# A first token list made in two parts, with its first 768 rows fetched under a narrower wait, and bracket counts kept from the search rounds

## The chip, the core and the metric

The kernel runs on one core of one Trainium2 chip. The metric is device time in microseconds (us) of one launch; lower is better. The time before is 1282.61 us, the median of three runs (1281.73 to 1284.68).

## What is computed

Two stages follow one another. The first is a channel attention over four batches (5056 tokens, 256 channels); the second sends every token of its output to exactly one of eight experts, in a greedy order with a fixed capacity, and runs that expert's two-layer network on it.

```python
qn = q / (np.linalg.norm(q, axis=1, keepdims=True) + 1e-06)
kn = k / (np.linalg.norm(k, axis=1, keepdims=True) + 1e-06)
s = kn.transpose(0, 2, 1) @ qn / tau
...
x = v @ a                                  # softmax of s; 4 x 5056 tokens, 256 channels
...
cap = N // E                               # 20224 tokens / 8 experts = 2528
logits = x @ w_gate
order = np.argsort(-logits.flatten())
for idx in order:                          # largest logit first
    tok, e = idx // E, idx % E
    if assigned[tok] >= 0 or counts[e] >= cap: continue
    assigned[tok] = e; counts[e] += 1
for e in range(E):
    mask = assigned == e
    out[mask] = np.maximum(x[mask] @ w1[e], 0.0) @ w2[e]
```

## The kernel before

**Attention and values.** `scores` and `softmax` make the four attention matrices. `x_tiles` (matmul L225, copy out of PSUM by ScalarE at L229) then multiplies values by them, eight 128-token rows at a time for each (batch, chunk) pair, and `store_x` (L235) sends the rows to a DRAM buffer `x_d` through ScalarE's DMA queue, four token rows per store. The last thirteen chunks stand in `TODO`; its last two are (2,4) and (3,0). They are computed while the first expert's tokens are being chosen. For the very last half chunk the loop stores two token rows at a time instead of four.

**Choosing the tokens of an expert (`route`).** The reference's greedy loop is done one full expert at a time, in eight passes p = 0 to 7; R = 8 - p experts are still open in pass p. A pass seeks the 32-bit score at which the first open expert is full. It is a search in eight rounds of four bits, four on the high half of the key and four on the low half. In each round VectorE compares all keys with 15 thresholds (L608), TensorE counts the hits per expert (`totals`: twenty matmuls at L577, one at L590), and VectorE reads the largest count (L597), marks the thresholds that are reached (`hit`, L601) and makes the next thresholds (L627, L634). I call the twenty-one matmuls of a round a **visit**. Behind the eight rounds stands a ninth visit: the keys are compared with the threshold that was found, once with "at least" and once with "above" (L651, L653), `totals` runs again, and from its two counts come the expert that is full and the room left in each (L658, L663). The mask of the chosen tokens follows at L719, the expert's number `ei` at L725. In the last pass (R = 1) nothing is searched.

**The list (`compact`).** From the mask a prefix sum (L514), a small matmul pair (L768, L769) and twenty tests (matmul L786, one per 128 list entries) give, for each of the 2528 list places, the row in `x_d` (`src`, L884) and in the output (`idx`, L897). For p = 0 ScalarE evaluates 11 of the tests (L804) and VectorE nine (L820); for the others ScalarE evaluates all.

**The experts.** Weights are fetched with an indirect DMA by GpSimd as soon as `ei` is known and the expert before has begun (`load_w`, L1051); the buffer of the second weight matrix must first be freed by the splitting of the previous one (L1060 on ScalarE, L1063 on VectorE). Token rows are fetched by indirect DMA, 128 per instruction (`load_x`, L1084), in chunks of up to four columns; the first expert's chunks have 2, 4, 4, 4, 4 and 2 columns (`FIRST_CUT`). The rows are turned, by TensorE for the first three chunks (`turn`: transposes L1237, ScalarE copy L1239, VectorE remainder L1242) and elsewhere by VectorE and DMA (`stage`, L1143). `layer1` (L1280, L1283, L1288) and `layer2` (L1314, L1321) then run, and GpSimd scatters the result rows (L1323).

**What sets the order.** All instructions are issued in the order in which the program emits them on their engine (`manual_schedule`). A planner (`Order`, with streams of generators) decides this order by a cost model: `ve(n)` is a VectorE instruction's cost, a yield of "P" asks for a place on TensorE, "A" on ScalarE, "W" waits for something to be emitted. Ties go to the stream with the lower priority number, and layer work comes first. A stream's next VectorE instruction is taken to be ready `DVE_TO_DVE` (70 ns) after its last.

**The seam between values and experts.** Behind the last value tile `actx.close()` gives back the buffers of the attention stage, among them the pool `vp` with the values and with the row buffers `xs` that `store_x` reads. Right after that the pool `ffx` is opened in the space that became free; `xg`, into which the rows are fetched, lies in it. The PSUM pools are exchanged in the same place.

```python
        actx.close()
        cctx.close()
        ffx = ctx.enter_context(tc.tile_pool(name="ffx", bufs=2))
        ...
        for c in range(2):
            load_x(0, c)
            while queue:
                gather()
        ...
        for i in range(START_TICKS):          # 24 matmuls on weights, result unused
            o.tick(200)
            PE.matmul(idle, lhsT=..., rhs=..., start=(i == 0), stop=(i == START_TICKS - 1))
        turn(0, 0, 0)
        turn(0, 0, 1)
```

The 24 matmuls (L1376) produce nothing. Chunk 1's transposes are emitted between `layer1(0, 0)` and `layer2(0, 0)`.

Of the kernel before, what the change touches and what calls it, by code (L numbers as in the profile page):

```python
# [8 lines left out]
F32 = mybir.dt.float32  # L9
# [21 lines left out]
LASTC = CAP - (NCOL - 1) * 128  # L31
GW = C + E
RB = 3
NACT = 11
# [14 lines left out]
HALF = 32768.0  # L49
CG = 128 // J  # L50
# [29 lines left out]
START_TICKS = 24  # L80
# [14 lines left out]
def attention_moe(ctx: ExitStack, tc: tile.TileContext, q, k, vt, tau, wg, w1t, w2t, tabs, out):  # L95
# [136 lines left out]
    def store_x(b, c, xs, t0, t1):  # L232
        r0 = (b * NCH + c) * CH
        rows = x_d[r0:r0 + CH].rearrange("(p t) c -> p t c", t=T)
        nc.scalar.dma_start(rows[:, t0:t1], xs[:, t0 % TH:t0 % TH + t1 - t0, 0:C])  # L235
# [283 lines left out]
    def route(p, R):  # L519
# [10 lines left out]
        else:  # L530
# [34 lines left out]
                            code9[:, None, 0:Q].to_broadcast([128, COLS, Q]), op=OP.is_equal)  # L565
            Ex = rtile("Ex", (128, J, E), F32R)
# [26 lines left out]
            def hits():  # L593
# [4 lines left out]
                hit = rtile("hit", (128, NT))  # L598
# [3 lines left out]
                r["n"] = n  # L602

# [8 lines left out]
            def search(keys):  # L612
                thr, cur = th0, None
                for i in range(NR):
                    yield from compare(keys, thr)
                    if 0 < i < NR - 1:
# [20 lines left out]

            yield from search(hi)
# [11 lines left out]
            yield ve(COLS, ptr=1)  # L650
            V.tensor_scalar(ge[:, :, 0], w.rearrange("p (g c) -> p g c", c=CG), th, None, op0=OP.is_ge)  # L651
            yield ve(COLS, ptr=1)
            V.tensor_scalar(ge[:, :, 1], w.rearrange("p (g c) -> p g c", c=CG), th, None, op0=OP.is_gt)  # L653
            yield from totals()
            tot = r["tot"]
            gen = rtile("gen", (128, E))
            yield ve(Q, psum=True)
            V.scalar_tensor_tensor(gen[:, 0:Q], tot[:, 0, :], 0.0, code9[:, 0:Q], op0=OP.is_ge, op1=OP.mult)  # L658
# [3 lines left out]
            yield ve(Q, psum=True)  # L662
            V.tensor_scalar(o9[:, 0, 0:Q], tot[:, 1, :], -1.0, None, op0=OP.mult)  # L663
# [57 lines left out]
        yield ve(COLS, 0.5)  # L721
        r["sc"] = prefix(r["mask"], "a")
# [6 lines left out]
        o.add(compact(p), lambda: COMPACT_PRIO)  # L729
# [26 lines left out]
    def compact(p):  # L756
        r = routed[p]
        sc = r["sc"]
# [13 lines left out]
        V.tensor_copy(first, po[:, 0:1])  # L772
        yield ve(COLS, psum=True)
        V.tensor_tensor(E_[:, 0:COLS], po[:, 128:128 + COLS], sc, op=OP.add)
        G = rtile("G", (128, NCOL * 128), BF)
        yield ve(NCOL * 128, 4, ptr=1)
        V.tensor_scalar(G, rgrid, first, None, op0=OP.is_ge)
# [4 lines left out]
        ended = []  # L782

# [5 lines left out]
        def by_act():  # L789
            todo = list(range(0, NACT, RB))  # L790
            held = []
            while todo or held:
                while todo and len(held) < 2:
                    g0 = todo.pop(0)
                    n = min(RB, NACT - g0)
# [5 lines left out]
                for i in range(n):  # L801
# [3 lines left out]
                                 accum_out=sgn[:, g0 + i:g0 + i + 1])  # L805
                yield "A", 200
                S.activation(ext[:, g0:g0 + n], pi[:, 0:n * W].rearrange("p (i w) -> p i w", w=W)[:, :, COLS:W], AF.Copy)
            ended.append(1)

        def by_dve():  # L810
            num = rtile("num", (128, NCOL))
            for g0 in range(NACT, NCOL, RB):
                n = min(RB, NCOL - g0)
# [3 lines left out]
                for i in range(n):  # L817
# [3 lines left out]
                                    op1=OP.add, accum_out=num[:, g0 + i:g0 + i + 1])  # L821
                yield ve(2 * n, psum=True)
                V.tensor_copy(ext[:, g0:g0 + n], pi[:, 0:n * W].rearrange("p (i w) -> p i w", w=W)[:, :, COLS:W])
            yield ve(NCOL)
            V.tensor_copy(at[:, NACT:NCOL], num[:, NACT:NCOL])
            ended.append(1)

        if p == 0:
# [4 lines left out]
            yield ve(NCOL)  # L833
            V.tensor_scalar(at[:, 0:NACT], sgn[:, 0:NACT], 0.5, COLS / 2.0, op0=OP.mult, op1=OP.add)
        for g in range(0, NCOL if p else 0, 2 * RB):
            yield "Q", min(2 * RB, NCOL - g) * 75
            held = []
            for g0 in range(g, min(g + 2 * RB, NCOL), RB):
                n = min(RB, NCOL - g0)
                pi = ps_t.tile([128, 512], F32, name="pt") if held else ps_c.tile([128, 512], F32, name="pi")  # L840
                tested(pi, g0, n)
# [378 lines left out]
    def turn(p, c, kb):  # L1220
# [27 lines left out]
        if kb == 1:  # L1248
            load_ahead(p, c)
# [243 lines left out]
```

## Time and profile before

| what | value |
|---|---|
| median of the three runs | 1282.61 us |
| the profiled execution, its own time | 1284.76 us |
| its span in the profile | 1282.8 us |
| mean granted TensorE clock in it | 0.997 of full speed |
| VectorE, ScalarE, GpSimd busy | 64%, 42%, 31% of the span |

The profile lists, per engine (PE is TensorE, PEld its weight loads, DVE VectorE, ACT ScalarE, POOL GpSimd, SP SyncE), when each instruction ran and what ended the idle time before it. Durations of single matmuls overlap, since TensorE pipelines them, so what a row of matmuls costs is read from the start of the next instruction. An arrow "<-" in brackets names the engine, tile and line whose end is taken to have released the wait; it is inferred from semaphores.

### The profile page before, as it was taken

What the parts mean: (1) busy time and instruction counts of PE and PEld (TensorE: products, weight loads), DVE (VectorE), ACT (ScalarE), POOL (GpSimd) and SP (SyncE); (2) the same over time, 40 slices, a digit from 0 to 9 for tenths busy, and PEclk for the clock granted to TensorE, in tenths of its full rate; (3) what the DMA queues carried; (4) which work ended last, traced back from release to release, by engine and by line L of the source; (5) the groups of instructions that cost most, each with busy time, mean ns of one, the idle gap of its engine ahead of it and who ended that gap; (6) DMA issues with size and microseconds to landing.
All of it is one profiled execution on the core that took longest, in us unless ns stands there. A gap on an engine that the chain in (4) does not pass through costs nothing.

```text
span 1282.8 us, 23360 instructions
## 1 busy us (share of the span) xinstructions
PE 1259.9 (98%) x8974; PEld 1123.1 (88%) x8974; DVE 814.9 (64%) x2013; ACT 540.3 (42%) x1217; POOL 395.4 (31%) x664
## 2 busy tenths in 40 slices
PE   7999999999899999999999999999999999999998
PEld 6889877888788989998989889988988998898998
DVE  6788596768478667867875876867644334434421
ACT  5567542335235343534442543443455333334331
POOL 1000001000343453254425533353344344335322
PEclk9999999999999999999999999999999999999999
DMA  8999982344224123232413431442243324313310
GB/s 298 365 380 340 366 324 110 132 148 185 75 84 143 49 88 114 84 91 72 161 42 95 148 102 38 143 152 70 76 147 119 111 82 144 106 63 105 111 62 33
DMA packets 67118, 178.29 MB, mean 139 GB/s; under 512 B 10944, under 2 KB 33344, under 8 KB 62400
## 3 DMA queue, kind: packets, MB, share of 16 engines
q1 hardware_dynamic: 39808, 97.54, 21.4%
q0 software_dynamic: 17664, 58.22, 13.9%
q10 hardware_dynamic: 9536, 21.06, 4.3%
q8 instruction: 70, 1.15, 0.4%
q14 instruction: 40, 0.33, 0.1%
HBM read 117.53 MB, written 59.24 MB: 138 GB/s over the span
## 4 chain that ended last, share of the span: by engine, by line
PE 85%; issue 5%; DVE 4%; DMA 2%; POOL 2%; ACT 1%; another core or an unknown queue 0%; POOLq 0%; SPq 0%; DVEq 0%; ACTq 0%
PE py L1314 31%; PE ph L1280 30%; PE s L304 8%; PE px L225 7%; PE pc L577 3%; PE px L268 2%; PE px L416 1%; POOL out_dram L1323 1%; DMA xg<-x_d,src 1%; DVE acc_q L314 1%; DVE acc_k L314 1%; DMA x_d<-xs 1%; DMA ua<-in_q_dram 1%; DVE hL L1288 0%; PE pi L786 0%
## 5 line engine op out<-in xcount | busy, mean ns | idle before, releaser
L1314 PE MATMUL py<-ua,hH 128*128 128x256 f32 (+1 forms) x2560 | 452.2, 280 | 0.0
L1280 PE MATMUL ph<-xH,ua 128*128 128x512 f32 (+3 forms) x1312 | 411.1, 388 | 4.8 <-DVE xs L1143 3.1
L1314 PEld LDWEIGHTS py<-ua,hH 128*128 128x128 f32 (+1 forms) x2560 | 389.1, 187 | 2.4
L1314 PE MATMUL py<-ua,hL 128*128 128x256 f32 (+1 forms) x1280 | 356.1, 278 | 0.0
L1288 DVE SCALAR_TENSOR_TENSOR hL<-ph,hH 128x512 fp32r<-128x512 f32 (+3 forms) x328 | 219.1, 669 | 171.8 <-ACT hH L1283 155.5
L1283 ACT ACTIVATE hH<-ph 128x512 fp32r<-128x512 f32 (+3 forms) x328 | 190.6, 582 | 235.8 <-PE ph L1280 209.3
L1280 PEld LDWEIGHTS ph<-xH,ua 128*128 128x128 f32 x1312 | 244.5, 189 | 51.4 <-DVE xs L1143 4.0
L1323 POOL DMA_INDIRECT out_dram<-y,idx x160 | 160.2, 1001 | 337.2 <-ACT y L1321 318.4
L1280 PE MATMUL ph<-xL,ua 128*128 128x512 f32 (+3 forms) x656 | 255.3, 389 | 0.8 <-DVE xL L1242 0.5
L1314 PEld LDWEIGHTS py<-ua,hL 128*128 128x128 f32 (+1 forms) x1280 | 239.1, 187 | 0.0
L1321 ACT ACTIVATE y<-py 128x256 f32<-128x256 f32 (+1 forms) x160 | 61.4, 384 | 311.2 <-PE py L1314 263.1
L1084 POOL DMA_INDIRECT xg<-x_d,src x160 | 162.5, 1016 | 94.1 <-issue 44.7
L304 PE MATMUL s<-ua 128*128 128x256 f32 (+1 forms) x640 | 145.2, 386 | 6.8 <-DMA ua<-in_q_dram 6.8
L304 PEld LDWEIGHTS s<-ua 128*128 128x128 f32 (+1 forms) x640 | 121.9, 193 | 26.7 <-issue 6.4
L1280 PEld LDWEIGHTS ph<-xL,ua 128*128 128x128 f32 x656 | 124.2, 189 | 23.4 <-DVE xL L1242 1.2
L313 ACT ACTIVATE sq<-ua 128x1024 f32<-128x1024 f32 (+1 forms) x80 | 76.3, 970 | 55.0 <-DMA ua<-in_k_dram 21.8
L1170 DVE TENSOR_TENSOR xL<-xT,xH 128x512 fp32r<-128x512 f32 (+1 forms) x68 | 44.9, 679 | 56.6 <-ACT xH L1167 56.2
L1095 POOL COPY spacer<-hH 1x1 f32<-1x1 f32 x130 | 27.1, 208 | 145.3 <-ACT hH L1283 140.1
L229 ACT ACTIVATE xs<-px 128x512 f32<-128x512 f32 x60 | 35.8, 597 | 76.2 <-PE px L225 76.2
L225 PE MATMUL px<-a,vr 128*128 128x256 f32 x256 | 59.4, 384 | 0.0
L334 POOL TENSOR_SCALAR ny<-ny 128x4 f32<-128x4 f32 x4 | 2.0, 504 | 182.8 <-ACT ny L333 182.8
L580 DVE TENSOR_TENSOR Dm<-pc,dmask 128x64 f32<-128x64 f32 (+3 forms) x63 | 12.6, 201 | 69.7 <-PE pc L577 47.2
(295 smaller groups left out, 1352.6 us busy)
## 6 DMA issues: line engine op xcount, KB each, us to landing
x_d<-xs ACTq DMA_DIRECT2D x39, 512.0 KB
ua<-in_k_dram SPq DMA_DIRECT2D x35, 512.0 KB
ua<-in_q_dram SPq DMA_DIRECT2D x35, 512.0 KB
via<-xs SPq DMA_DIRECT2D x33, 512.0 KB
xT<-via SPq DMA_DIRECT2D x132, 128.0 KB
vr<-in_vt_dram SPq DMA_DIRECT2D x14, 1024.0 KB
ua<-in_vt_dram SPq DMA_DIRECT2D x4, 1024.0 KB
xg<-x_d,src POOLq DMA_INDIRECT x160
```

Source lines behind the costliest of these rows:

```text
L225: mm = PE.matmul(px[:, i * C:i * C + width], lhsT=vs[b, c][:, kb, t + i, :], rhs=a_f[b][:, kb, 0:width], start=(kb == 0), stop=(kb == 1))
L304: newest[0] = PE.matmul(sb[:, ib * C:(ib + 1) * C], lhsT=kt[:np_, t, ib * 128:(ib + 1) * 128], rhs=qt[:np_, t, :], start=(first and t == 0 ...
L313: S.activation(sq[:n, t0:t1], t_[:n, t0:t1], AF.Square)
L577: PE.matmul(D, lhsT=ge[:, g], rhs=oh[:, cs_, 0:Q], start=(g == 0), stop=(g == COLS // CG - 1))
L1084: P.indirect_dma_start(out=xg[:n, i, :], out_offset=None, in_=x_d, in_offset=bass.IndirectOffsetOnAxis(ap=idx[:n, col:col + 1], axis=0))
L1170: V.tensor_tensor(xL[:, kb, 0:k * 128].rearrange("p (i t e) -> p i t e", i=k, t=4), rows, xH[:, kb, 0:k * 128].rearrange("p (i t e) -> p i ...
L1280: PE.matmul(ph[:, 0:nt], lhsT=l[:, w], rhs=x_[:, kb, 0:nt], start=(i == 0), stop=(i == 5))
L1283: S.activation(hH[:, fb, 0:nt], ph[:, 0:nt], AF.Relu)
L1288: V.scalar_tensor_tensor(hL[:, fb, 0:nt], ph[:, 0:nt], 0.0, hH[:, fb, 0:nt].bitcast(F32), op0=OP.max, op1=OP.subtract)
L1314: PE.matmul(py[:n, 0:C], lhsT=l[:, fb, tk], rhs=w[:, d], start=(j == 0), stop=(j == 23))
L1321: S.activation(y[:n], py[:n, 0:C], AF.Copy)
L1323: sd = P.indirect_dma_start(out=out, out_offset=bass.IndirectOffsetOnAxis(ap=idx[:n, col:col + 1], axis=0), in_=y[:n], in_offset=None)
```

## The change

**The list of expert 0 in two parts.** `compact(0)` first copies the mask without the tokens that the last one and a half chunks of values produce (all of (3,0), the second half of (2,4); `LATE_PAIR = 5`), makes a list of this reduced mask for six columns only (`HEAD = 6`, 768 places), then subtracts what is listed from the mask and makes the other 14 columns from the rest. `listed` is the old body of `compact` with a column range; three tests of the head and eight of the rest go to ScalarE. The six fetches of the head are declared independent of the stores of those last values. The last half chunk is stored with one store of four token rows.

**The ninth visit.** In each round ScalarE copies the counts out of PSUM (`S.activation(seen...)`), and a new stream `keep` runs three VectorE instructions on them: counts whose threshold was reached are shifted down by `HIT`, a minimum over the shifted ones and a maximum over the others are carried to the next round. Behind round eight the two results stand in `seen[0]`; the two comparisons and the visit are gone.

**The seam.** The 24 idle matmuls are gone. `turn_both` turns both halves of chunk 0 with four transposes in one PSUM tile. Chunk 1 is turned at steps 4 and 7 of `layer1(0, 0)`.

**Smaller edits.** The streams `compact` and `keep` are `quick` (ready without the 70 ns). `turn` first drives a list stream that reads the same PSUM tile to the end of its reading.

```diff
+            def keep():
+                for k in range(2 * NR):
+                    while len(rounds) <= k:
+                        yield "W", 0
+                    now_, then = seen[k % 2], seen[(k + 1) % 2]
+                    yield ve(NT * Q)
+                    V.scalar_tensor_tensor(now_[:, 1:NT + 1], rounds[k][:, :, None].to_broadcast([128, NT, Q]), -HIT,
+                                           now_[:, 1:NT + 1], op0=OP.mult, op1=OP.add)
+                    k0 = 0 if k else 1
+                    yield ve((NT + 1) * Q)
+                    V.tensor_reduce(then[:, 0], now_[:, k0:NT + 1].rearrange("p k r -> p r k"), axis=AX.X, op=OP.min)
+                    yield ve((NT + 1) * Q)
+                    V.tensor_reduce(then[:, NT + 1], now_[:, 1:NT + 2].rearrange("p k r -> p r k"), axis=AX.X, op=OP.max)
+                    r["kept"] = k + 1
...
+                while r["kept"] < len(rounds) - 1:
+                    yield "W", 0
+                S.activation(seen[len(rounds) % 2][:, 1:NT + 1], r["tot"][:, 0:NT], AF.Copy)
...
             th = r["cur"]
-            V.tensor_scalar(ge[:, :, 0], w.rearrange("p (g c) -> p g c", c=CG), th, None, op0=OP.is_ge)
-            V.tensor_scalar(ge[:, :, 1], w.rearrange("p (g c) -> p g c", c=CG), th, None, op0=OP.is_gt)
-            yield from totals()
+            rounds.append(r["new"])
+            while r["kept"] < 2 * NR:
+                yield "W", 0
-            V.scalar_tensor_tensor(gen[:, 0:Q], tot[:, 0, :], 0.0, code9[:, 0:Q], op0=OP.is_ge, op1=OP.mult)
+            V.scalar_tensor_tensor(gen[:, 0:Q], seen[0][:, 0], -HIT, code9[:, 0:Q], op0=OP.is_ge, op1=OP.mult)
...
     def compact(p):
+        mask = routed[p]["mask"]
+        if p > 0:
+            sc = prefix(mask, "a")
+            yield from listed(p, sc, 0, NCOL)
+            return
+        head = rtile("mem")
+        V.tensor_copy(head, mask)
+        c0 = (NCH - 1) * T + LATE_PAIR * 16
+        V.memset(head[32:64, c0:c0 + 16], 0.0)
+        V.memset(head[64:128, c0:c0 + 16], 0.0)
+        sc = prefix(head, "a")
+        yield from listed(p, sc, 0, HEAD)
+        V.tensor_scalar(sc, sc, routed[p]["first"], None, op0=OP.add)
+        V.scalar_tensor_tensor(head, sc, HEAD * 128.0, head, op0=OP.is_le, op1=OP.mult)
+        V.tensor_tensor(head, mask, head, op=OP.subtract)
+        sc = prefix(head, "a")
+        yield from listed(p, sc, HEAD, NCOL)
...
         def fetch(i, col, n):
+            rows = P.indirect_dma_start(...)
+            if p == 0 and col < HEAD:
+                for st in late_stores:
+                    tc.declare_no_dep(rows.ins, st.ins, reason="at least 768 rows of a list lie outside the last rows")
...
+    def turn_both():
+        xg = xgs[0, 0]
+        xH, xL = xts[0, 0] = (ffx.tile([128, 2, 512], F32R, name="xH"), ffx.tile([128, 2, 512], F32R, name="xL"))
+        pt = ps_t.tile([128, 512], F32, name="pt")
+        for i in range(cuts[0][0]):
+            for kb in range(2):
+                PE.transpose(pt[:, kb * nt + i * 128:kb * nt + (i + 1) * 128].bitcast(F32R),
+                             xg[:, i, kb * 128:(kb + 1) * 128].bitcast(F32R), identr)
+        for kb in range(2):
+            rows = pt[:, kb * nt:(kb + 1) * nt]
+            S.activation(xH[:, kb, 0:nt], rows, AF.Copy)
+            V.tensor_tensor(xL[:, kb, 0:nt], rows, xH[:, kb, 0:nt].bitcast(F32), op=OP.subtract)
+        o.pe += 1500
...
-                if i + 1 == len(TODO) and t >= TH:
-                    store_x(b, c, xs, t, t + 2)
-                elif t % TH == 2:
-                    store_x(b, c, xs, t - 2, t + 2)
+                if t % TH == 2:
+                    st = store_x(b, c, xs, t - 2, t + 2)
+                    if (b, c) == PAIRS[LATE_PAIR][1] or (b, c) == PAIRS[LATE_PAIR][0] and t >= TH:
+                        late_stores.append(st)
...
-        for i in range(START_TICKS):
-            o.tick(200)
-            PE.matmul(idle, lhsT=wt[0, 0][0][:, 0:128], rhs=wt[0, 0][0][:, 512:1024], start=(i == 0),
-                      stop=(i == START_TICKS - 1))
-        turn(0, 0, 0)
-        turn(0, 0, 1)
+        turn_both()
...
-            h[0] = layer1(p, 0, {**pieces} if p == 0 else {2: [turn_at(1, 0)], 7: [turn_at(1, 1)], **pieces})
+            h[0] = layer1(p, 0, {4: [turn_at(1, 0)], 7: [turn_at(1, 1)]} if p == 0 else {2: [turn_at(1, 0)], 7: [turn_at(1, 1)], **pieces})
...
-                    turn(p, 1, 0)
-                    turn(p, 1, 1)
```

More of the change, by code (lines that the diff above doesn't have):

```diff
@@ L565, in route @@
                             code9[:, None, 0:Q].to_broadcast([128, COLS, Q]), op=OP.is_equal)
+            seen = [eq.bitcast(F32).rearrange("p r c -> p (r c)")[:, i * 320:i * 320 + (NT + 2) * Q]
+                    .rearrange("p (k r) -> p k r", r=Q) for i in range(2)]
+            yield ve(Q)
+            V.tensor_scalar(seen[0][:, NT + 1], ne[:, 0, 0:Q], -1.0, None, op0=OP.mult)
+            rounds = []
+            r["kept"] = 0
+            def keep():
[12 more added lines that the diff above has]
+                    r["kept"] = k + 1
             Ex = rtile("Ex", (128, J, E), F32R)
@@ L615, in search @@
                     yield from compare(keys, thr)
+                    if r["new"] is not None:
+                        rounds.append(r["new"])
                     if 0 < i < NR - 1:
@@ L636, in search @@
                 r["cur"] = cur
+            o.add(keep(), lambda: EDGE_PRIO).quick = True
+            r["new"] = None
             yield from search(hi)
@@ L775, in compact @@
         G = rtile("G", (128, NCOL * 128), BF)
-        yield ve(NCOL * 128, 4, ptr=1)
-        V.tensor_scalar(G, rgrid, first, None, op0=OP.is_ge)
+        yield ve(nc_ * 128, 4, ptr=1)
+        V.tensor_scalar(G[:, 0:nc_ * 128], rgrid[:, 0:nc_ * 128], first, None, op0=OP.is_ge)
         W = COLS + 2
@@ L789, in by_act @@
         def by_act():
-            todo = list(range(0, NACT, RB))
+            todo = list(range(0, nact, RB))
             held = []
@@ L889, in compact @@
+        V.copy_predicated(src[:, cs_], early[:, cs_], w3_[:, cs_])
+        for col in range(c0, c1):
+            r["src", col] = src
+        if not short:
+            r["time"] = o.pe
+            done["idx", p] = True
+            lists.append(p)
         bt = rtile("bt", (128, NCOL))
-        yield ve(NCOL)
-        V.tensor_scalar(bt, src, float(NCH * CH), None, op0=OP.is_ge)
+        yield ve(nc_)
+        V.tensor_scalar(bt[:, cs_], src[:, cs_], float(NCH * CH), None, op0=OP.is_ge)
         for b_ in range(2, B):
-            yield ve(NCOL)
-            V.scalar_tensor_tensor(bt, src, float(b_ * NCH * CH), bt, op0=OP.is_ge, op1=OP.add)
@@ L901, in attention_moe @@
+        for col in range(c0, c1):
+            r["idx", col] = idx
+        if not short:
+            done["out", p] = True
+    reading = []
     spacer = rt.tile([1, 2], F32, name="spacer")
@@ L1232, in turn @@
         xH, xL = xts[p, c]
+        while reading:
+            reading[0].step()
         o.flush(turned[0])
```

149 lines of the change are left out of this document (83 added, 66 removed).

## The prediction

> **What bounds the kernel now.** I read the page's first rows and its chain of work first, then the stages by window, then the seam in order of time.
>
> ```profile
> span 1282.8 us, 23360 instructions
> PE 1259.9 (98%) x8974; PEld 1123.1 (88%) x8974; DVE 814.9 (64%) x2013; ACT 540.3 (42%) x1217; POOL 395.4 (31%) x664
> PE 85%; issue 5%; DVE 4%; DMA 2%; POOL 2%; ACT 1%; another core or an unknown queue 0%; POOLq 0%; SPq 0%; DVEq 0%; ACTq 0%
> ```
>
> TensorE is the bound nearly everywhere: 98% busy, 85% of the chain. So an edit is worth what it takes from TensorE's own work or from its few empty places. Of these the seam between values and experts is the largest behind the start:
>
> ```profile
> 287.00:322.60 35.60, 35.50 (x228) 30.33 (x226) 31.55 (x95) 19.38 (x52) 0.00 (x0) 1.00 0.50 193
> 322.60:332.06 9.46, 7.11 (x50) 5.52 (x50) 4.13 (x13) 0.98 (x2) 4.22 (x5) 1.00 0.27 91
> 332.06:343.00 10.94, 9.53 (x80) 8.89 (x79) 5.21 (x13) 3.97 (x10) 2.84 (x5) 0.84 0.12 37
> 582.31:704.25 121.94, 121.25 (x987) 109.91 (x986) 89.14 (x258) 49.32 (x126) 49.01 (x80) 1.00 0.30 95
> ```
>
> The columns behind the stretch are its length, then busy time of PE, PEld, DVE, ACT, POOL, the granted clock, DMA share and GB/s. The 7.11 us of PE in the second row are mostly the 24 idle matmuls. In the third the granted clock is 0.84: 10.94 x 0.16 = 1.75 us lost. In order of time the seam reads:
>
> ```profile
> 319.78 2.81 PE L225 MATMUL px<-a_last,vr 128*128 128x256 f32 x12
> ...
> 322.62 0.60 ACT L229 ACTIVATE xs<-px 128x512 f32<-128x512 f32 x1 [1.13 <-PE px L225]
> 323.25 0.33 ACTq L235 DMA_DIRECT2D x_d<-xs  x1
> 323.27 1.20 PE L1376 MATMUL ph<-ua 128*128 128x512 f32 x4 [0.69 <-ACT xs L229]
> ...
> 326.63 0.95 POOL L1084 DMA_INDIRECT xg<-x_d,src  x1 [40.59 <-DVE Ex L586]
> ...
> 330.64 0.28 PE L1237 MATMUL pt<-identr,xg 128*128 128x128 f32 x1 [0.74 <-DMA xg<-x_d,src]
> ...
> 332.06 0.35 PE L1280 MATMUL ph<-xH,ua 128*128 128x256 f32 x1
> ...
> 342.60 0.53 PE L1237 MATMUL pt<-identr,xg 128*128 128x128 f32 x4 [1.28 <-DVE xL L1242]
> ```
>
> I call the end of the last value matmul T = 319.78 + 2.81 = 322.59. The first fetch starts 4.04 us later, the second column's rows are there at T + 8.05, layer 1 starts at T + 9.47. The DVE instruction that the fetch's row names belongs to pass 1 and writes nothing that the fetch reads, and the fetch's list had long been ready (its row is below): what it waited for is the last store, issued at 323.25.
>
> **Does the fetch really go ahead?** That decides 10 us, so it comes first. The change takes away the dependence of the six fetches on the last stores through `x_d`. But there is a second one. `xg` lies in `ffx`, opened in space that `vp` has just given back, and two rows show what a first instruction in such a new pool waits for:
>
> ```profile
> L904 POOL MEMSET ge<- 128x2560 bf16 x1 | 2.2, 2231 | 26.1 <-DVE L L421 26.1
> ```
>
> The memset of `ge`, the first one in the pool `rt`, waits 26.1 us for a DVE copy out of `turned`. It shares no data with it; what they have in common is that `turned` belongs to a pool that was closed just before. Likewise the first idle matmul above (323.27) reads only weights and still waits for ScalarE's last copy out of `px`, a tile of the closed PSUM pool. So a new pool's tiles wait for the last users of the closed pools. The users of `vp` are the last value matmuls, ScalarE's last copy into `xs`, and the last stores that read `xs`. The diff leaves `ffx` and its place as they are, and a declared independence of two DMAs doesn't speak of pools. I forecast that **the fetches still start behind the last store**, and the list's two parts buy nothing.
>
> **The sum, part by part.**
>
> *Ninth visit.* The chain of waits in the value stage gives the price of a visit:
>
> ```profile
> 221.03 14.01 PE px L225 x64
> ...
> 242.18 3.07 PE px L225 x14
> 245.25 0.58 PE pc L577 x20
> 245.84 1.38 PE px L225 x6
> 247.21 0.06 PE pc L590
> 247.27 3.07 PE px L225 x14
> ...
> 893.20 0.51 PE pc L577 x20
> ...
> 899.50 0.51 PE pc L577 x20
> ```
>
> From 242.18 to 247.27 are 5.09 us for 20 value matmuls, which alone take 20 x 14.01 / 64 = 4.38: a visit costs 0.71, of which 0.13 is L590. Later passes have fewer columns; the last two visits of the last search (893.20, 899.50) cost 0.51 + 0.13 = 0.64. Seven visits go, 2 x 0.71 + 5 x 0.64 = **-4.6 us**, all of it TensorE's own time.
>
> *Kept counts.* Per round three DVE instructions and one ACT copy come in. None of them is in the trace; nearest are these:
>
> ```profile
> L597 DVE TENSOR_REDUCE mxs<-pc 128x15 f32<-128x120 f32 (+3 forms) x56 | 13.3, 238 | 25.1 <-PE pc L590 24.9
> L627 DVE SCALAR_TENSOR_TENSOR thr<-n_hit,pre 128x120 int16<-128x120 f32 x28 | 7.9, 282 | 0.7
> L850 ACT ACTIVATE ext<-pi 128x6 f32<-128x6 f32 (+1 forms) x28 | 4.9, 174 | 0.0
> 263.87 1.48 DVE L608 TENSOR_TENSOR ge<-low,thr 128x1200 bf16<-128x1200 int16 x2
> ...
> 266.68 0.23 DVE L580 TENSOR_TENSOR Dm<-pc,dmask 128x64 f32<-128x64 f32 x1 [1.19 <-PE pc L577]
> ```
>
> DVE: 0.282 + 2 x 0.238 = 0.76 us a round, 6.1 a pass; ACT: between these 0.17 and the 0.60 of a 128x512 copy (322.62 above) a round. In pass 0 the 0.76 fit into the 1.19 us in which DVE waits for the visit (last row), so rounds stay at 5.1 us. In the expert stages DVE is busy 89 of 122 us (582.31 above); it has room for 6.1 more. But its queue is in order: a round's counts or a layer remainder (L1288) can stand behind the new ones and TensorE behind those. What that costs today when it happens is a row pair in the chain:
>
> ```profile
> 438.39 0.20 DVE Dm L580
> ...
> 439.51 1.26 PE ph L1280 x9
> ```
>
> TensorE lost 0.9 us of 1.1 there. From nothing to one such place more in each of the six later passes (5.4 us) are the ends; I take **+0.7**, near the lower end, since such a place is rare now at 73% load. The ACT copy's cover is ACT's 60% of idle time; without it the delay is one copy, 0.6 us at most. The copy adds one wait: the next visit overwrites the PSUM tile that it reads. On TensorE the whole layer work is queued behind that visit, but the next comparison lies in between (1.48 us at 263.87), so I cost it at nothing.
>
> *The list.* A second round of prefix, small matmuls and closing arithmetic is added. Its cover:
>
> ```profile
> 282.39 0.33 DVE L719 TENSOR_TENSOR mk<-mk,m 128x160 f32<-128x160 f32 x1
> ...
> 285.67 1.01 DVE L777 TENSOR_SCALAR G<-rgrid,first 128x2560 bf16<-128x2560 int16 x1
> ...
> 310.20 0.18 DVE L884 COPY_PREDICATED src<-early,w__2722 128x20 int32<-128x20 int32 x1
> ```
>
> ```profile
> 284.91 0.09 PE pc L769
> ```
>
> From mask to the tests' input are 3.3 us, and the closing arithmetic is some 17 instructions of 0.18: a second time, 6.4 us, against the 12.2 between 310.38 and T. Beyond that cover it would push the seam by the rest. On TensorE it is one more matmul pair: **+0.1**. The twenty tests stay twenty, shared between ACT and DVE as before.
>
> *Seam.* (a) The last store carries 512 KB instead of 256. The page's highest rate is 380 GB/s in a slice, at which 256 KB take 0.7 us; a part overlapped with the store before: fetch at T + 4.5 (ends +0 and +0.7). (b) The fetches keep their place in POOL's queue, nothing is moved past them; from the first one to the second column 4.01 us as now (330.64 - 326.63): T + 8.5. (c) `turn_both` makes both halves at once: transposes 0.4, ACT copy 0.4, layer 1 at T + 9.3 against T + 9.47 now: -0.2. What stands late next is the second half's remainder on DVE, as now. (d) Chunk 1's turns move into layer 1, where its six fetches, landed by about T + 13.5, are in time: the 1.28 us wait (342.60) goes, -1.1 with what it drags along. (e) One visit of pass 1 ran inside the idle matmuls for nothing; now it stands on the path: +0.7. (f) Without the idle matmuls TensorE is empty from T to T + 8.5. Now a thin stretch costs 1.75; I take 0.8 more, between nothing and a second 1.75. Together: -0.2 - 1.1 + 0.7 + 0.8 = **+0.2** (-1.5 to +2).
>
> The Trainium skill, "TensorE: Matmul & The Clock Gate", Part 1, says that an idle window of about 3.4 us halves the clock and about as much sustained work is needed to get it back. The trace agrees: 1.75 us lost are 3.5 us at half clock. By that rule the empty 8.5 us make the drop certain and a loss of 1.7 to 3.4 an estimate of the page's; term (f) would be 0 to +1.7.
>
> *Weights.* `load_w` for the next expert is issued at a stage's start if `ei` is known; its second fetch then blocks POOL until the split frees the buffer, with row fetches behind it. The first row is an `ei` that comes late enough; the other two are the worst case now, in the last stage but one:
>
> ```profile
> 712.42 0.15 DVE L725 SCALAR_TENSOR_TENSOR ei<-es,pcol 128x1 int32<-128x1 f32 x1
> ...
> 1066.20 0.96 POOL L1051 DMA_INDIRECT ub<-in_w2t_dram,ei  x1 [7.62 <-DVE ua L1063]
> ...
> 1074.00:1084.00 10.00, 7.70 (x38) 6.30 (x37) 4.46 (x7) 1.80 (x4) 4.39 (x7) 0.83 0.48 152
> ```
>
> It cost 2.3 us of empty TensorE and 10 x 0.17 = 1.7 of clock. A pass loses a visit and its wait, about 6 us (899.50 - 893.20). So `ei` of pass 4, at 712.42 now, falls before the stage's start at 704.25 (the end of the fourth window above), and that stage gets this block too: 0 to 4.0, I take **+0.7**.
>
> Sum: -4.6 + 0.7 + 0.1 + 0.2 + 0.7 = -2.9. The profiled execution took 1284.76 us (span 1282.8 and 1.96 around it): 1281.9 for its like. It is 2.15 above the median of the runs; from the median, 1282.61 - 2.9 = **1279.7 us**.
>
> **The rivals.**
>
> 1. *The fetches do go ahead.* For it: the diff builds it, and the code after the seam counts on 1.5 us. Against: the two rows on new pools. Layer 1 would start at T + 1.4 (transposes, ACT's last value copy, its own copy): -8 against T + 9.47, the clock loss of 1.75 gone and, of the terms above, -1.1 and +0.7: -10.1 in place of +0.2. Time 1269.4. Chance 0.10.
> 2. *Half of it:* the pool holds the fetch behind ScalarE's last copy (323.22), not behind the store. The fetch starts at about T + 1.0 instead of T + 4.5: 3.5 less, 1276.2. Chance 0.08.
> 3. *Slower:* the weight block. If the stages of pass 2 and of pass 3 both get it at its full price, 2 x 4.0 in place of 0.7, the time is 1279.7 - 0.7 + 8.0 = 1287.0. It decides for slower once new blocks take over 6.2 us together (0.7 + 2.9 + 2.6). For it: `ei` moves across a stage's start. Against: the two stages before the one above have the same block, and their whole idle time on TensorE is 0.7 and 0.9 us:
>
> ```profile
> 823.23:943.20 119.97, 119.29 (x945) 107.52 (x945) 77.52 (x219) 53.93 (x155) 48.54 (x81) 1.00 0.33 107
> 943.20:1055.60 112.40, 111.52 (x745) 100.96 (x745) 50.48 (x107) 51.07 (x140) 47.09 (x82) 1.00 0.35 116
> ```
>
> Chance 0.10.
>
> My forecast has 0.72, with some 2.5 us of its own either way. What a measurement tells from no change is 0.2%, 2.6 us: 1280.0. Of 0.72 I put 0.41 below that and 0.31 within. With rivals 1 and 2: faster 0.59, same 0.31, slower 0.10. The range of eight in ten takes in the forecast's bounds and rival 2 and leaves rival 1 and most of rival 3 out: 1274.0 to 1284.8.
>
> **What would show it.** L577 with 1120 matmuls instead of 1260. The first L1084 about 4.5 us behind the last L225; if it stands ahead of the last L235, my reading of the pools is wrong. An empty TensorE of some 8 us between L225 and L1237, and a granted clock below one behind it. No wait ahead of chunk 1's turns. L1051 with 7 to 9 us of idle time before its second fetch in the stage that starts near 702. Expert stages longer than now by over 1 us, with DVE named, would show the kept counts dearer than I take them.

## The result: 1.0% slower, and the profile after

The changed kernel takes 1296.24 us (median of four runs, 1295.95 to 1296.92) against 1282.78 beside it: a ratio of 1.0101, 95% interval 1.0088 to 1.0113. The forecast of 1279.7 and the whole range are missed, on the wrong side.

The first rows of the page of the changed kernel:

```profile
span 1293.9 us, 23241 instructions
PE 1265.0 (98%) x8805; PEld 1124.4 (87%) x8805; DVE 848.4 (66%) x2182; ACT 551.6 (43%) x1273; POOL 396.2 (31%) x662
```

TensorE runs 169 matmuls fewer than before (8805 for 8974) and is busy 5.1 us longer. That is the first thing to stop at: its empty time has grown too, by 6.0 us (22.9 to 28.9), much of it where the 24 idle matmuls stood, but fewer matmuls take longer. Lines have moved: the visit is now L602 and L615, the fetch L1153, the turns L1311 and L1333, layer 1 L1372, layer 2 L1405, the last store L238.

The seam by window, answering to the three rows of before (columns as there; T, the end of the last value matmul, is 322.30 + 1.54 = 323.84, for 322.59 before):

```profile
323.90:332.94 9.04, 0.96 (x5) 0.62 (x4) 0.30 (x2) 0.96 (x2) 3.79 (x4) 0.69 0.30 102
332.94:343.00 10.06, 10.05 (x82) 9.72 (x83) 7.17 (x19) 4.64 (x12) 1.90 (x2) 0.77 0.14 41
```

and in order of time:

```profile
322.30 1.54 PE L228 MATMUL px<-a_last,vr 128*128 128x256 f32 x6
...
324.51 0.33 ACTq L238 DMA_DIRECT2D x_d<-xs  x1
327.93 0.95 POOL L1153 DMA_INDIRECT xg<-x_d,src_h  x1 [44.92 <-DMA x_d<-xs]
...
330.84 0.47 PE L1333 MATMUL pt<-identr,xg 128*128 128x128 f32 x2 [6.93 <-DMA xg<-x_d,src_h]
...
332.94 0.58 PE L1372 MATMUL ph<-xH,ua 128*128 128x256 f32 x1 [0.47 <-ACT xH L1337]
```

The fetch still stands behind the last store, at T + 4.09; TensorE is empty for 6.93 us. So far it is the forecast. The loss shows where nothing of the change runs at all. The stage of pass 7 has no routing, no kept counts and no list beside it. Here is a window of it, cut at the same matmuls in both kernels, first in the trace of before, then in that of after:

```profile
1170.28:1247.13 76.85, 76.69 (x482) 68.73 (x481) 33.03 (x50) 29.98 (x57) 27.63 (x49) 1.00 0.26 84
```

```profile
1178.69:1257.60 78.91, 78.82 (x482) 69.93 (x481) 33.01 (x50) 29.86 (x57) 27.66 (x49) 1.00 0.24 81
```

The same 482 matmuls, nearly the same work on the other engines, the clock 1.00 in both, and 2.06 us more. The chain of waits shows both layers slower, again before and then after:

```profile
1191.11 10.92 PE py L1314 x96
1202.02 9.60 PE ph L1280 x42
```

```profile
1199.91 11.31 PE py L1405 x96
1211.22 9.80 PE ph L1372 x42
```

A second-layer matmul comes every 10.92 / 96 = 113.8 ns before and every 117.8 after. What the change did to these matmuls is not in any line of layer 1 or 2: its small new tiles (`src_h`, `idx_h`, a second buffer of `hit`) make the pool `rt` 128 bytes per partition larger, and every tile of `ffx`, opened behind it (x, h, y), lies 128 bytes higher. The weights stay where they were. That this move is the cause is tested next.

### The profile page after: what moved, and what is told of

It reads as the page before. It is cut to its first block, busy times and chain, and to the rows that moved or that the text cites. A ratio compares the mean times of both kernels' runs of the same rounds, so it can differ in the third digit from the quotient of the medians.

```text
span 1293.9 us, 23241 instructions
## 1 busy us (share of the span) xinstructions
PE 1265.0 (98%) x8805; PEld 1124.4 (87%) x8805; DVE 848.4 (66%) x2182; ACT 551.6 (43%) x1273; POOL 396.2 (31%) x662
## 4 chain that ended last, share of the span: by engine, by line
PE 82%; DVE 8%; issue 5%; POOL 2%; DMA 2%; ACT 1%; POOLq 0%; another core or an unknown queue 0%; SPq 0%; DVEq 0%; ACTq 0%
PE py L1405 30%; PE ph L1372 30%; PE s L307 8%; PE px L228 6%; PE px L271 2%; PE pc L602 2%; PE px L419 1%; POOL out_dram L1414 1%; DMA xg<-x_d,src 1%; DVE acc_q L317 1%; DVE acc_k L317 1%; DVE hL L1380 1%; DMA ua<-in_q_dram 0%; DVE m L536 0%; PE pi L846 0%
## 5 line engine op out<-in xcount | busy, mean ns | idle before, releaser
L1405 PE MATMUL py<-ua,hH 128*128 128x256 f32 (+1 forms) x2560 | 459.7, 281 | 0.0
L1372 PE MATMUL ph<-xH,ua 128*128 128x512 f32 (+3 forms) x1312 | 416.1, 392 | 4.5 <-DVE hL L1380 2.7
L1405 PEld LDWEIGHTS py<-ua,hH 128*128 128x128 f32 (+1 forms) x2560 | 390.8, 186 | 2.4
L1405 PE MATMUL py<-ua,hL 128*128 128x256 f32 (+1 forms) x1280 | 358.2, 280 | 0.0
L1372 PEld LDWEIGHTS ph<-xH,ua 128*128 128x128 f32 x1312 | 245.9, 190 | 55.1 <-DVE hL L1380 4.5
L1372 PE MATMUL ph<-xL,ua 128*128 128x512 f32 (+3 forms) x656 | 257.1, 392 | 0.4 <-DVE xL L1242 0.2
L1414 POOL DMA_INDIRECT out_dram<-y,idx x154 | 153.7, 998 | 331.2 <-ACT y L1412 305.1
L1405 PEld LDWEIGHTS py<-ua,hL 128*128 128x128 f32 (+1 forms) x1280 | 238.3, 186 | 0.0
L1153 POOL DMA_INDIRECT xg<-x_d,src x154 | 158.9, 1032 | 53.3 <-issue 44.0
L1372 PEld LDWEIGHTS ph<-xL,ua 128*128 128x128 f32 x656 | 124.6, 190 | 25.8 <-DVE xL L1242 2.0
L228 PEld LDWEIGHTS px<-a,vr 128*128 128x128 f32 x256 | 47.2, 190 | 6.0
```

The lines of the kernel that those rows point to most:

```text
L228: mm = PE.matmul(px[:, i * C:i * C + width], lhsT=vs[b, c][:, kb, t + i, :], rhs=a_f[b][:, kb, 0:width], start=(kb == 0), stop=(kb == 1))
L1153: rows = P.indirect_dma_start(out=xg[:n, i, :], out_offset=None, in_=x_d, in_offset=bass.IndirectOffsetOnAxis(ap=routed[p]["src", col][:n, ...
L1372: PE.matmul(ph[:, 0:nt], lhsT=l[:, w], rhs=x_[:, kb, 0:nt], start=(i == 0), stop=(i == 5))
L1405: PE.matmul(py[:n, 0:C], lhsT=l[:, fb, tk], rhs=w[:, d], start=(j == 0), stop=(j == 23))
L1414: sd = P.indirect_dma_start(out=out, out_offset=bass.IndirectOffsetOnAxis(ap=routed[p]["idx", col][:n, col:col + 1], axis=0), in_=y[:n], i ...
```

## The experiments

Three theories stood against each other. **P**: TensorE runs slower because its operands have moved against each other. **D**: the kept counts load VectorE and ScalarE and slow TensorE. **S**: the time went at the seam. Ratios are to the kernel before on the same chip, with 95% intervals.

### Moving the pool back, and moving it in the kernel before

r1_home, from the changed kernel (two dead tiles are used again, which frees 192 bytes):

```diff
-PAD_X = 16
+PAD_X = 32
...
-        early = rtile("early", (128, NCOL), I32)
+        early = k1
...
-        w3_ = rtile("w3_", (128, NCOL), I32)
+        w3_ = k2
```

The other three change `PAD_X` alone, the size in 4-byte words of a tile ahead of the others in `ffx`: r2_before_moved is the kernel before with 48 in place of 16, r3_after_512 and r4_after_256 are the changed kernel with 112 and 48.

> The changed kernel with nothing but its tile places altered: two dead tiles are used again (early in k1, w3_ in k2) and pad_x grows by 64 bytes, so that every tile of pool ffx (xg, xH, xL, hH, hL, y) lies where it lay before the change, 128 bytes lower than in the changed kernel. Theory P (TensorE is slower because the change pushed ffx up by 128 bytes): the x96 py groups of the stage of pass 7 go back from 11.31 to 10.92 us, the stage from 78.91 to 76.85 us, the whole by about 8 x 2 = 16 us at most and 10 at least, so 1280 to 1286 us. Theory D (the kept counts' work on VectorE and ScalarE, or their reads and writes, slows TensorE): no change, 1295 to 1297 us. Theory S (the time went at the seam, the 2.0 us wait for chunk 2 and the half clocks): no change, 1295 to 1297 us.

> The kernel before with pad_x 128 bytes larger, so that every tile of ffx lies where the changed kernel has it; not one instruction is added or taken away. Theory P: py x96 11.3 us in place of 10.92 in the stage of pass 7, and the whole 10 to 16 us longer, 1293 to 1299 us. Theories D and S: nothing of theirs is in it, 1282 to 1284 us.

> The changed kernel with pad_x 384 bytes larger: ffx lies 512 bytes above its place before the change. Theory P with a period of 512 bytes: as r1_home, 1280 to 1286 us. Theory P with another period, or where the distance alone counts: 1290 to 1300 us. Theories D and S: 1295 to 1297 us.

> The changed kernel with pad_x 128 bytes larger: ffx lies 256 bytes above its place before the change. Theory P with a period of 256 bytes: as r1_home, 1280 to 1286 us; with a longer period: neither this nor that is fixed, 1280 to 1300 us. Theories D and S: 1295 to 1297 us.

| run | ffx against its old place | ratio |
|---|---|---|
| r1_home | 0 | 0.9991 (0.9982 to 1.0000) |
| r2_before_moved | +128 bytes | 1.0120 (1.0104 to 1.0135) |
| r3_after_512 | +512 | 0.9981 (0.9972 to 0.9991) |
| r4_after_256 | +256 | 0.9983 (0.9974 to 0.9993) |

The same window of the stage of pass 7 in r2_before_moved, then in r1_home:

```profile
1175.40:1254.30 78.90, 78.81 (x482) 69.92 (x481) 33.02 (x50) 30.01 (x56) 27.64 (x49) 1.00 0.25 82
```

```profile
1161.30:1238.15 76.85, 76.68 (x482) 68.73 (x481) 33.02 (x50) 29.90 (x57) 27.65 (x49) 1.00 0.27 85
```

The kernel before takes on the changed kernel's pace when its tiles move, without one instruction more, and the changed kernel takes on the old one when they move back. The move of `ffx` is shown to be the cause, as P has it, and D and S fall as the main cause. The two effects multiply to the result: 1.0120 x 0.9983 = 1.0103, measured 1.0101.

### Which places are good

e10, e12 and e13 are the kernel before with `PAD_X` = 80, 32 and 64; e5 moves the second layer's weights instead (the kernel before, with `early` and `w3_` as in r1_home):

```diff
-PAD_W = 8
-PAD_X = 16
+PAD_W = 40
+PAD_X = 32
```

> The kernel before with pad_x 256 bytes larger and nothing else: the place of ffx at which r4_after_256 and e7, e8 and e9 ran. If a move by 256 bytes costs TensorE nothing (theory P with a period of 256): ratio 1.000 within 0.15%, py x96 10.92 us; it is then the kernel before at the place of those runs, for a comparison stage by stage. If every move costs: 1.003 to 1.012.

> The kernel before with pad_x 64 bytes larger: the distance between x and the first layer's weights, modulo 256, goes from 0 to 64, that between the hidden values and the second layer's weights from 64 to 128. Known of theory P1 so far: first layer fast at 0, slower at 128; second fast at 64, slower at 192. If half of the 256 bytes are good and half bad with the same rule for both layers (0 and 64 good, 128 and 192 bad): first layer fast, second slow, about 1.005. If the layers have rules of their own: open, 1.000 to 1.012.

> The kernel before with pad_x 192 bytes larger: distances modulo 256 of 192 (first layer) and 0 (second). By the rule of e12 (0 and 64 good, 128 and 192 bad): first layer slow, second fast, 1.003 to 1.007. If the layers have rules of their own: open, 1.000 to 1.012.

> The kernel before with the second layer's weight tiles ua2 and ua3 (and ub0, ub1) 128 bytes higher and the tiles of ffx where they lay (two dead tiles used again take back the 128 bytes). Which operand's place counts? If the distance of the two operands of a matmul does (theory P1), the second layer is hit as in r2_before_moved and the first isn't: py x96 11.3 us in place of 10.92, ph x42 9.60 as before, about 1.005 to 1.010 of the time before. If the place of the hidden values alone does (P2), py stays at 10.92 and the time is that of before within 0.2%.

| run | moved | ratio | py x96 us | ph x42 us |
|---|---|---|---|---|
| e10_before_256 | ffx +256 | 0.9994 (0.9985 to 1.0004) | 10.92 | 9.60 |
| e12_before_64 | ffx +64 | 1.0140 (1.0120 to 1.0160) | 11.39 | 9.62 |
| r2_before_moved | ffx +128 | 1.0120 (1.0104 to 1.0135) | 11.31 | 9.80 |
| e13_before_192 | ffx +192 | 1.0169 (1.0149 to 1.0188) | 11.51 | 9.81 |
| e5_w2_moved | second weights +128 | 1.0052 (1.0036 to 1.0068) | 11.30 | 9.55 |

The py and ph columns are rows of the chain of waits in the stage of pass 7, as quoted above for before and after. e12 and e13 are two executions each. A move by 256 bytes changes nothing and one by 128 does, so the period is 256 bytes. Within it the old place is the best of the four that were run. The first guess of a rule was that offsets 0 and 64 between a layer's two operands are good and 128 and 192 bad, for both layers. e12 still fits it layer by layer (first layer at 64 nearly untouched, second at 128 slow), though at 1.0140 in place of the expected 1.005. e13 breaks it: there the second layer is at offset 0, which should be good, and is the slowest of all. In e5 the hidden values stay in place and the second layer is slow all the same, while the first isn't: it is not the place of the hidden values alone that counts. That it is how the two operands lie to each other is supported by m2 below, where all of them move together and nothing changes.

### The disputed cost by itself

These three kernels leave out all but layer blocks, and each was executed once: with x and h at eight offsets against the weights (m1), the same with everything 128 bytes higher (m2), and at the four pairs of offsets of full kernels with the full strides (m3):

```diff
+    for i, a in enumerate("abcdefgh"):
+        cases[a] = [pool.tile([128, 1024 + 64], F32R, name=f"{n}{a}")[:, 8 * i:8 * i + 1024] for n in ("xH", "xL", "hH", "hL")]
...
+                        for l, x_ in ((wH, xH), (wH, xL), (wL, xH)):
+                            PE.matmul(ph, lhsT=l[:, w], rhs=x_[:, kb], start=(i == 0), stop=(i == 5))
```

> A kernel of matmuls alone (it leaves out the whole computation): the 48 of a first-layer block (128x128 weights from wH or wL, 512 columns of xH or xL) and the 96 of four second-layer rows (128x128 of hH or hL, 256 columns of wH or wL), at eight distances of x or h from w modulo 256 bytes (a 0, b 32, c 64, d 96, e 128, f 160, g 192, h 224), first with no other engine at work, then with the copies of ScalarE and VectorE beside them. If the distance of the two operands sets the rate: first layer fastest at a (227 ns from start to start), then c 229, e 231, g 232; second layer fastest at c (113 to 114), slower at a, e, g (118 to 120), in the quiet part too. If it is a collision with the copies: all eight alike in the quiet part. If it is something else in the full kernel (addresses of far tiles, the routing): all eight alike in both parts.

> m1_places with every tile 128 bytes higher, the eight distances unchanged. If the distance alone counts: the same eight rates within 1 ns. If the places themselves count: the order of the eight cases changes.

> Matmuls alone again (the whole computation is left out), now with the full kernel's strides (a row of 512 hidden values per 128 features) and in its order: a first-layer block of 48, then four second-layer rows of 24, at the four pairs of distances that were run in full kernels (0 and 64 as before the change, 64 and 128, 128 and 192 as after it, 192 and 0), twice over. If the distances alone set the rates: first layer 227, 229, 230, 232 ns from start to start, second 113 to 114, 119, 118, 120, so that the x96 rows read 10.9, 11.4, 11.3 and 11.5 us. If the fast pace of the second layer needs something else of the full kernel: 117 to 120 in all four.

In m1, with the copies beside it, 48 first-layer matmuls from start to start at offsets 0, 32, 64, 128 and 192 (the first column is the stretch, the second its length; the counts take in a neighbour or two):

```profile
193.57:204.50 10.93, 10.93 (x51) 9.02 (x50) 4.68 (x7) 4.19 (x7) 0.00 (x0) 1.00 0.00 0
204.50:215.70 11.20, 11.20 (x50) 8.99 (x48) 5.58 (x9) 4.78 (x8) 0.00 (x0) 1.00 0.01 1
215.70:226.70 11.00, 11.00 (x50) 9.01 (x48) 5.51 (x9) 4.78 (x8) 0.00 (x0) 1.00 0.00 1
237.91:249.11 11.20, 11.20 (x50) 9.01 (x48) 5.53 (x9) 4.78 (x8) 0.00 (x0) 1.00 0.01 1
260.35:271.54 11.19, 11.19 (x49) 9.02 (x48) 5.52 (x9) 4.80 (x8) 0.00 (x0) 1.00 0.01 1
```

That is 227.7, 233.3, 229.2, 233.3 and 233.1 ns a matmul. The quiet part, in which ScalarE and VectorE stand still, gives the same numbers for the seven offsets other than 0 (at offset 32, worked out from the starts, 233.4 in both), so no collision with their work is needed. The block at offset 0 is not quiet there: it runs first, with tiles still being filled, its first matmuls every 427 ns and the later ones every 227. m2 agrees within 0.2 ns at every offset of the part with copies, so the offset counts and not the place. Offset 0, which the kernel before has in the first layer and the change took away, is the best here and in m3 (227.3). The order of the others isn't settled by the offset alone: 64 reads 229.2 in m1 and 233.4 in m3, with the same first-layer matmuls and a second layer between them.

The pace of the second layer in full kernels is met only in part. Alone it runs at 117.3 to 120.0 ns at all eight offsets in m1, and in m3 at 117.8, 118.6, 117.8 and 119.8. The slow ones of full kernels are met (117.8 for 11.31 / 96 = 117.8 in r2, 118.6 for 11.39 / 96 = 118.6 in e12, 119.8 for 11.51 / 96 = 119.9 in e13), but the 113.8 of the old place, which was expected at offset 64, never appears. The starts in the full traces show why an average misleads: at the old place there are two paces, one of 113 to 114 ns and one of 117 to 118. In the kernel before, behind 465 us, the intervals read 118, 120, 120, 123, 118, 114, 113, 113, 114, then a visit cuts in, and then 118, 118, 117 and so on to the end of the row. Share of second-layer intervals of at most 115 ns:

| run | pass 1 | pass 3 | pass 5 | pass 7 |
|---|---|---|---|---|
| e10_before_256 | 0.37 | 0.46 | 0.85 | 0.96 |
| r1_home | 0.59 | 0.67 | 0.96 | 0.96 |
| e5_w2_moved | 0.11 | 0.04 | 0.40 | 0.40 |
| r2_before_moved | 0.04 | 0.03 | 0.04 | 0.04 |
| the changed kernel | 0.07 | 0.23 | 0.04 | 0.04 |

In the even passes the old place has 0.35 to 0.96 (r1_home: 0.70, 0.35, 0.36 and 0.96 in passes 0, 2, 4 and 6), the changed kernel at most 0.13 and r2 at most 0.05. So the old place lets TensorE fall into the fast pace and the new one hardly does. What starts the fast pace, and why e5 reaches it at times where r2 doesn't at the same offset, stays open.

### The parts of the change, at a good place

e7 keeps only the counts, e8 only the list and the new start; both with ffx at +256. The single last store and the smaller edits stay in both.

In e7, from the changed kernel (chunk 1's turns, too, go back behind `layer1(0, 0)`, and the six fetches are not declared independent):

```diff
-NACT = {HEAD: 3, NCOL - HEAD: 8}
+NACT = {NCOL: 11}
...
-        if p > 0:
+        if p >= 0:
...
-        turn_both()
+        for i in range(START_TICKS):
...
+        turn(0, 0, 0)
+        turn(0, 0, 1)
```

In e8, from the changed kernel (the copies, the kept counts and their reading go):

```diff
-            o.add(keep(), lambda: EDGE_PRIO).quick = True
...
+            yield ve(COLS, ptr=1)
+            V.tensor_scalar(ge[:, :, 0], w.rearrange("p (g c) -> p g c", c=CG), th, None, op0=OP.is_ge)
+            yield ve(COLS, ptr=1)
+            V.tensor_scalar(ge[:, :, 1], w.rearrange("p (g c) -> p g c", c=CG), th, None, op0=OP.is_gt)
+            yield from totals()
```

> The kept counts in place of the ninth visit alone: one list, the idle matmuls and the turns as in the kernel before; ffx 256 bytes above its place before the change, where r4_after_256 ran at full rate. By the terms of the prediction -4.6 + 0.7 + 0.7 = -3.2 us, a ratio of 0.9975 (0.996 to 0.998). If the kept counts' own work on VectorE delays TensorE more than forecast: 0.998 to 1.001. If the parts don't add up, it differs from r4_after_256 less e8_list_alone by over 1 us.

> The list in two parts with the early fetch and the new start of the first chunk alone, and the ninth visits as in the kernel before; ffx 256 bytes above its place before the change. By the terms of the prediction +0.1 + 0.2 = +0.3 us, a ratio of 1.000. If the wait for chunk 2 (2.0 us at 354.9) and its half clock take back what the seam gives: 1.000 to 1.002. If the seam's gain (chunk 1's start is 2.8 us nearer in r1_home) stays to the end: 0.998 to 0.999.

e7: 0.9992 (0.9983 to 1.0001); e8: 1.0046 (1.0032 to 1.0061); both together, in r4: 0.9983. e7 lies above the 0.996 to 0.998 of the prediction's terms, in the range that was named for kept counts that delay TensorE more than forecast; e8 lies above every range named for it. The parts don't add up (-0.8 and +4.6 thousandths, -1.7 together). e7's loss isn't in the expert stages: from the start of pass 1's layers to that of pass 6's it takes 591.58 us, 1.9 less than e10. But its layer 1 starts at T + 12.1, for T + 9.6 in e10; why is open. One piece is seen in the stage of pass 6: an empty place that is 2.13 us in e8 and 2.32 in e10, but 0.86 in e7 and 0.89 in r4. So it gets shorter with the kept counts, and the list has no part in it. In e8, then e10, then e7, then r4:

```profile
1078.07 0.50 PE L1345 MATMUL ph<-xH,ua 128*128 128x512 f32 x1 [2.13 <-DVE hL L1353]
```

```profile
1073.31 0.50 PE L1280 MATMUL ph<-xH,ua 128*128 128x512 f32 x1 [2.32 <-DVE hL L1288]
```

```profile
1073.06 0.50 PE L1373 MATMUL ph<-xH,ua 128*128 128x512 f32 x1 [0.86 <-DVE hL L1381]
```

```profile
1071.04 0.50 PE L1372 MATMUL ph<-xH,ua 128*128 128x512 f32 x1 [0.89 <-DVE hL L1380]
```

Against e10, r4 gains 2.9 us between the second and the third chunk of that stage, where e10's half clock falls away too. That is single execution against single execution, and the traced one of e10 lies 2.8 us above the median of its ten (1281.03 for 1278.24). Over the stretch from pass 1 to pass 6, e8 takes 2.6 us more than e10 and r4 2.9 less (596.13, 593.52 and 590.67 us). Two visits more fall into this stretch in e8 (820 matmuls of its L580, for 780 of e10's L577), 1.3 us at the prediction's 0.64; the rest was not followed further.

### Is it the pool that holds the fetch?

e9, from r4_after_256 (`ps_1`, `ps_2` and `ps_t` are opened like `ffx`):

```diff
+                if i == 1 and t == 2:
+                    store_x(3, 0, xs, 0, TH)
+                    store_x(3, 0, xs, TH, T)
+                    store_x(2, 4, xs, TH, T)
...
-        ffx = ctx.enter_context(tc.tile_pool(name="ffx", bufs=2))
+        ffx = ctx.enter_context(tc.tile_pool(name="ffx", bufs=2, reuse_waits="tile"))
```

e11, from e9:

```diff
         load_x(0, 2)
+        while queue:
+            gather()
...
         turn_both()
+        idle = ps_1.tile([128, 512], F32, name="ph")
+        for i in range(6):
+            PE.matmul(idle[:, 0:256], lhsT=wt[0, 0][0][:, 0:128], rhs=wt[0, 0][0][:, 512:768], start=(i == 0), stop=(i == 5))
```

> r4_after_256 with pools ffx, ps_1, ps_2 and ps_t opened so that each tile waits for the users of its own bytes alone and not for the last user of the closed pools; and the rows of the last stores filled once, early, from another tile, since the fetch's source must hold numbers everywhere when it starts. If the release of the closed pool held the fetch back, as the prediction's step (a) has it: first fetch before 316 us, in place of about 4 us behind the last value matmul, the empty stretch of 6.9 us at the first transpose gone, 5 to 10 us less than r4_after_256, ratio to before 0.990 to 0.994. If the fetch waits for something else (the stores through x_d): first fetch behind 325 us and the time of r4_after_256, 0.998.

> e9_tile_waits with the four fetches of chunk 2 issued right behind the first six, in place of one at a time between the scatters, and six idle matmuls behind the first transposes to fill the 1.1 us in which TensorE waits for the first copies. If the wait for chunk 2 (0.99 us at 346.7 in e9) and the half clock of 3.4 us (1.7 us lost) behind the empty 1.1 us are what is left at the seam: 1.5 to 3 us less than e9, ratio 0.991. If the fetches of chunk 2 now hold up the first scatters and the weights: the time of e9 or above, 0.993 to 0.995.

The seam of e9, in order of time:

```profile
313.99 0.97 POOL L1153 DMA_INDIRECT xg<-x_d,src_h  x1 [31.40 <-DVE hit L628]
...
323.31 0.48 PE L1333 MATMUL pt<-identr,xg 128*128 128x128 f32 x4
...
324.07 0.33 ACTq L238 DMA_DIRECT2D x_d<-xs  x1
...
324.88 0.39 PE L1372 MATMUL ph<-xH,ua 128*128 128x256 f32 x1 [1.09 <-ACT xH L1337]
```

The first fetch stands 10 us ahead of the last store, the rows wait for TensorE and not it for them, and of 6.9 empty us 1.09 are left. The ratio is 0.9930 (0.9916 to 0.9944), 0.5% less than r4. So it was the release of the closed pool that held the fetch, as the prediction argued from its two rows on new pools. e11 reads 0.9916 (0.9902 to 0.9930), not told apart from e9: its seam is better, its clock 1.00 where e9's was 0.91, as these windows of e9 and then e11 show,

```profile
323.00:343.00 20.00, 18.76 (x158) 17.38 (x158) 13.37 (x38) 7.26 (x18) 5.13 (x8) 0.91 0.17 56
828.00:840.00 12.00, 10.76 (x89) 9.36 (x88) 8.01 (x25) 5.46 (x20) 6.76 (x13) 1.00 0.51 154
```

```profile
323.00:343.00 20.00, 19.23 (x173) 17.50 (x172) 13.61 (x41) 7.43 (x19) 7.93 (x10) 1.00 0.26 82
828.00:840.00 12.00, 9.85 (x78) 8.78 (x79) 8.10 (x25) 4.58 (x19) 4.52 (x9) 0.86 0.42 133
```

but, 2.3 us ahead of e9, it comes early to pass 4's layers, waits 2.47 us there for VectorE (1.24 in e9), and runs at half clock behind it. A gain upstream turned into a wait.

## Why the prediction was wrong

**The step that failed** is a clause: "The diff leaves `ffx` and its place as they are". The statement that opens the pool is unchanged; its address isn't, and no term of the sum allowed TensorE's own pace to change. What it is in the hardware that the offset acts on stays open. The move costs 1.2% of 1278 us, 15 us (r2). Of it the second layer has about 9.6: its mean interval is 2.5 ns longer over the eight passes than in e10, times 3840 matmuls. The first layer has the rest; 3 to 4.6 ns on 1968 matmuls are 6 to 9, and 2 to 3 are given back in pass 6, where e10's wait of 2.32 us is 1.32 in r2 and no half clock follows it.

**The sum without that step comes out, in part by luck.** At a good place the change gives -0.17% (-0.26 to -0.07, r4), -0.9 to -3.3 us, for a forecast of -2.9; r3 gives -0.19% and r1_home -0.09%. But a list that cost 2 us more than its term stands against a block that didn't come and a gain in pass 6 that nobody forecast. Term by term:

- *Ninth visit and kept counts.* 1120 matmuls at L602, as said. From the start of pass 1's layers to that of pass 6's, r4 gains 2.9 us on e10 and runs 80 of these matmuls fewer, four visits, which at 0.64 are 2.6. The counts cost about nothing there. The counts' own size was right: 0.24 + 0.31 + 0.30 = 0.84 us of VectorE a round for the 0.76 taken.

```profile
L586 DVE TENSOR_REDUCE eq<-eq 128x8 f32<-128x128 f32 (+7 forms) x56 | 17.1, 306 | 1.6
L588 DVE TENSOR_REDUCE eq<-eq 128x8 f32<-128x128 f32 (+3 forms) x56 | 16.8, 300 | 0.0
L582 DVE SCALAR_TENSOR_TENSOR eq<-hit,eq 128x120 f32<-128x120 f32 (+3 forms) x56 | 13.2, 236 | 0.6 <-ACT eq L630 0.6
```

- *The list, +0.1,* was too small. From the first value matmul to T are 239.6 us before, 240.9 in the changed kernel and 238.7 in e7, which has the counts but one list: the second part of the list costs some 2.2. Two new waits stand ahead of T in the changed kernel, 1.66 us together; the cover on VectorE didn't cover TensorE, which has a small matmul of the list and one of the next search in its queue ahead of the next values.

```profile
293.98 0.16 PE L826 MATMUL pc<-cb,before 128*128 128x1 bf16 x1 [1.05 <-DVE cb L820]
...
313.39 0.33 PE L615 MATMUL pc<-Ex,ones_q 128*128 128x128 f32 x1 [0.61 <-DVE Ex L611]
```

- *The seam.* Fetch at T + 4.09 (forecast 4.5), layer 1 at T + 9.10 (9.3), no wait for chunk 1: right. The clock behind it is 0.77 over 10.06 us, 2.3 us lost, 0.6 more than before for the 0.8 taken. What is late next was missed: chunk 2's fourth fetch, for which TensorE waits 2.00 us in this trace, with half clock behind it; in r4 the same wait is 0.94 and the clock stays at 1.00.

```profile
356.90 0.28 PE L1311 MATMUL pt<-identr,xg 128*128 128x128 f32 x1 [2.00 <-DMA xg<-x_d,src]
```

```profile
356.12 0.28 PE L1311 MATMUL pt<-identr,xg 128*128 128x128 f32 x1 [0.94 <-DMA xg<-x_d,src]
```

- *Weights, +0.7,* had the wrong sign of shift. `ei` of pass 4 comes at 721.85, later and not earlier, since pass 1's routing takes longer: 120.6 us from the first `ei` to the second for 106.3. Both parts have a share in that, since the counts alone (e7) make it 114.9 and the list alone (e8) 120.5. The fetch at 724.75 waits for nothing.

```profile
721.85 0.15 DVE L753 SCALAR_TENSOR_TENSOR ei<-es,pcol 128x1 int32<-128x1 f32 x1
```

```profile
724.75 1.18 POOL L1121 DMA_INDIRECT ub<-in_w2t_dram,ei  x1 [0.30 <-issue]
```

**The rivals.** The mechanism of rival 1 is real but needs a narrower release: e9 takes 0.5% from r4, 7 us, for the 10 worked out. Its layer 1 starts at T + 1.47, as the rival had it (1.4), but the clock loss that was to go stays (0.91 over 20 us, 1.8 us). Rival 2 fell: the fetch stands behind the store. Rival 3 had the right side for a wrong reason; its weight block didn't come. None of the three looked at where the tiles lie.

## What to carry to other kernels

Ask of every diff which tiles it moves: a new 24-byte tile shifts all that is opened behind it. Before a result of under 2% is put down to the logic of an edit, compare a stage that the edit doesn't touch, matmul for matmul; if its pace has changed at the same clock, put the old addresses back and time again. And where a DMA is declared free of a data dependence, look for the second wait that the reuse of its buffer brings.

## What was not expected of the hardware

- TensorE's pace depends on the offset, modulo 256 bytes, between the two operands of its matmuls in SBUF: 227.7 ns at offset 0, with the copies beside it, and 229 to 234 at the seven others, with or without them, for 128x512 (m1). The Trainium skill, "TensorE: Matmul & The Clock Gate", "Step-by-step: what each phase is for", says that loading the next tile's weights takes no SBUF read bandwidth from the running matmul. The runs neither confirm nor refute this: they show that the two operands' places act on the pace, not whether it is through the weight load or through something else.
- The second layer has two paces, 113 to 114 and 117 to 118 ns, and a visit in between throws it from the fast one into the slow one: so it went at all 20 places of the trace of before where a visit cut into the fast pace (by the means of the last four intervals ahead of it and the first five behind).
